# k and v of the first batch loaded into all 128 partitions instead of two half-partition pieces

## The chip, the cores and the metric

The kernel runs on one core of one Trainium2 chip. The metric is the device time of one execution in microseconds (us), the median over runs. The profile shows one execution, in us from the start of its span.

## What is computed

A linear attention with a norm over each head is followed by a token-mixing and a channel-mixing layer (a ResMLP block). Cut to what matters, with B = 8 batches, H = 8 heads, S = 576 tokens, D = 64:

```python
kv  = einsum('bhsd,bhse->bhde', k, v)              # per head, 64 x 64
o   = einsum('bhsd,bhde->bhse', q, kv)
o   = o / sqrt(mean(o*o, -1) + 1e-6) * g_norm
x   = o.transpose(0, 2, 1, 3).reshape(B, S, H*D)   # 8 x 576 x 512
a1  = alpha1 * x + beta1
u   = x + lam * einsum('ts,bsd->btd', w_tok, a1)
a2  = alpha2 * u + beta2
out = u + lam * (maximum(a2 @ w_ch1, 0) @ w_ch2)   # 512 -> 2048 -> 512
```

All inputs and the output are float32. q, k and v are each [8, 8, 576, 64].

## The kernel before

**One batch after the other.** For every batch the kernel makes kv for the eight heads, multiplies q by it, norms, mixes tokens (`tok_groups`), transposes (`ut_groups`) and runs the two channel products (`ch1_groups`, `ch2_groups`). While a batch is in its channel products, the next one is prepared. From batch 1 on, k and v come in one transfer of 1 MB each (`load_kv`), with 512 tokens over 128 partitions and 64 tokens in a tail tile.

**The first batch is different.** Its loads have no earlier batch to run beside, and they are cut into two halves of four heads, a = 0 and a = 1 (`HALVES`). `load_first(a)` (L508) loads k and v of a half. A head has 576 tokens, which are spread over 64 partitions with 9 tokens each, so a partition takes one unbroken piece of 9 x 64 floats (2304 bytes) of a head. `nine(tile, a, g)` (L463) is the view of that: partition half g of the tile holds two heads. Heads 4a and 4a+1 lie in partitions 0 to 63, heads 4a+2 and 4a+3 in partitions 64 to 127. Each (tile, a, g) is a transfer of its own, of 288 KB to 64 partitions: eight in all. The order of the loads on the SP queue is, for a = 0 and then a = 1: k (two transfers), v (two), q of the half (`load_main`, L493, 512 KB), and behind q of half 0 the last 64 tokens of q for all eight heads (`load_tail`, L500, 128 KB, into 64 partitions of `qft`). Then comes `moe_w_tok` (L1120, 1152 KB, and L1123, 144 KB).

**What the first batch does with it.** `kv_first` (L601) makes kv of a half: 36 small matmuls (72 instructions in the profile, since float32 takes two), each with 64 rows and 64 columns of the array, so that four of them sit in the array together. The head picks the rows (partition half of the input) and the columns (partition half of the PSUM output). ACT copies the results onto the diagonal blocks of `kv32` (L618): block r holds two heads, one in each partition half and column half. `qt_first` (L623) transposes q by matmuls with the identity: `pair(pr)` (L625, matmuls at L631) takes two heads into one block of `qt32`, `tail(a)` (L639, L645) takes the last 64 tokens. `qkv_groups` (L745) with `f32` (L767, matmuls at L771) then multiplies each block of `qt32` by the same block of `kv32`, 128 output columns for two heads at once, and writes them into PSUM side by side. Behind that follow the norm on ACT and DVE, and the transposes of `moe_w_tok` (`wt_groups`, L1151, matmuls at L1161), the token mix of batch 0 (`tok_first`, L905) and its transposes (L940), and the first channel product (L988).

**The order is made by a planner.** `Prog.op` records operations with an engine, an estimated cost, keys that are read and written, and for transfers an estimated `dma_us`. `Prog.schedule` (L169) is a list scheduler that runs them on its own clock and so fixes every engine's order when the program is built; `Prog.plan` (L122) repeats it eight times with other priorities and keeps the best. On its clock transfers pass through one pipe:

```python
dma_free = max(dma_free, t + 0.6) + pick.lat     # lat is dma_us
pick.end = dma_free + 2.0
```

**Filler matmuls.** As long as the first channel product has not started on the planner's clock, PE is never left idle in the plan: where no operation is ready, one filler matmul (`warm`, L1341 and L1342, 0.22 us on that clock) on a tile of zeros is written into PE's order. It is a fixed instruction: the chip runs it whether or not the data has come by then.

**The SP queue.** The loads are chained (`P.chain`), so they are issued in program order. `load_kv(1)` overwrites the buffers of half 0 and so waits for its matmuls; `load_q(1)` waits for the transposes of q.

Of the kernel before, what the change touches and what calls it, by code (L numbers as in the profile page):

```python
# [395 lines left out]
def bass_transnormer_attn__then__resmlp_affine_kernel(  # L396
# [15 lines left out]
    with ExitStack() as stack:  # L412
        P = Prog(nc, stack)

        def sb(name, shape, dt):
            return stack.enter_context(nc.sbuf_tensor(name, shape, dt))

        ident = sb("ident", [128, 128], F32)
# [23 lines left out]
        kv32 = kvd[:].rearrange("p h i d -> p (h i d)").bitcast(F32).rearrange(  # L442
            "p (r e) -> p r e", r=4)
# [16 lines left out]
        wst = hst[:, 0:2304].rearrange("p (c s) -> p c s", c=4)  # L460
        wst2 = hst[0:64, 2304:2880]

        def nine(tile, a, g):  # L463
            return tile[64 * g:64 * g + 64, a].rearrange("p h c d -> p (h c d)")[
                :, 0:1152].rearrange("p (h c d) -> p h c d", h=2, c=9)

        def flat(ap):
            return ap.rearrange("p h d -> p (h d)")
# [7 lines left out]
        def act_us(n):  # L476
            return 0.19 + n / 1200.0
# [4 lines left out]
        def act_dve(n, mode=1):  # L482
            return {"ACT": act_us(n), "DVE": dve_us(n, mode)}
# [4 lines left out]
        def copy(e, out, in_):  # L488
            if e is nc.scalar:
                return e.activation(out, in_, ACT.Identity)  # L490
            return e.tensor_copy(out=out, in_=in_)
# [8 lines left out]
        def load_tail(tile, key, src, b, lo, eng="SP"):  # L500
            P.op(eng, 0.6, lambda e: e.dma_start(
                tile[lo:lo + 64, :, :], src[b, :, 512:576, :].rearrange("h s d -> s h d")),
                w=[key], dma_us=0.75)

        HALVES = (slice(0, 4), slice(4, 8))
        ALL = (slice(0, 8),)

        def load_first(a):  # L508
            for key, src, tile in (("kf", k, kf), ("vf", v, vf)):
                for g in range(2):  # L510
                    P.op("SP", 0.45, lambda e, src=src, tile=tile, g=g: e.dma_start(
                        nine(tile, a, g).rearrange("p h c d -> p h (c d)"),
                        src[0, 4 * a + 2 * g:4 * a + 2 * g + 2].rearrange(
                            "h (p c) d -> p h (c d)", c=9)),
                        w=[(key, a)] if g == 0 else [(key + "g", a)], dma_us=1.05)

        def load_kv(b, go=()):
            j = (b + 1) % 2
            for tile, tl, src, n in ((kf, kft, k, "kf"), (vf, vft, v, "vf")):
                P.op("SP", 0.6, lambda e, tile=tile, src=src: e.dma_start(  # L520
                    tile[:, j].rearrange("p h c d -> p h (c d)"),
                    src[b, :, 0:512, :].rearrange("h (p c) d -> p h (c d)", c=4)),
                    r=go, w=[(n, j), (n + "g", j)], dma_us=3.8)
# [77 lines left out]
        def kv_first():  # L601

            def group(a):
                t = P.ptile(2)

                def f(e):
                    for c in range(9):
                        for h in (0, 2, 1, 3):
                            g, r = h // 2, slice(64 * (h % 2), 64 * (h % 2) + 64)
                            m = e.matmul(t.ap(r)[:, g, 0:64], nine(kf, a, g)[:, h % 2, c, :],  # L610
                                         nine(vf, a, g)[:, h % 2, c, :],
                                         start=(c == 0), stop=(c == 8), skip_group_check=True)
                    return m
                P.op("PE", 1.8, f, r=[(n, a) for n in ("kf", "kfg", "vf", "vfg")], w=[t])
                for h in range(2):
                    rows = slice(64 * h, 64 * h + 64)
                    P.op("ACT", act_us(128), lambda e, h=h, rows=rows: copy(
                        e, kv32[rows, 2 * a:2 * a + 2, 64 * h:64 * h + 64],  # L618
                        t.ap(rows)[:, :, 0:64]), r=[t, "kvz"], w=[("kv32", a, h)])
            for a in range(2):  # L620
                yield lambda a=a: group(a)

        def qt_first():  # L623

            def pair(pr):  # L625
                t = P.ptile(1)

                def f(e):
                    for c in range(4):
                        for h in range(2):  # L630
                            m = e.matmul(t.flat(slice(64 * h, 64 * h + 64))[  # L631
                                :, 128 * c:128 * c + 128], qf[:, 2 * pr + h, c, :], ident[:],
                                start=True, stop=True)
                    return m
                P.op("PE", 0.95, f, r=["ident", ("qf", pr // 2)], w=[t])
                P.op(act_dve(512), 0, lambda e: copy(e, qt32[:, pr, 0:512], t.flat()),
                     r=[t], w=[("q32", pr)])

            def tail(a):  # L639
                t = P.ptile(1)  # L640

                def f(e):
                    for pr in range(2):
                        h = 4 * a + 2 * pr
                        m = e.transpose(t.flat()[:, 64 * pr:64 * pr + 64],  # L645
                                        qft[0:64, h:h + 2, :].rearrange("p h d -> p (h d)"),
                                        ident[0:64, 0:64])
                    return m
                P.op("PE", 0.28, f, r=["ident", "qft0"], w=[t])
                P.op(act_dve(128), 0, lambda e: copy(  # L650
                    e, qt32[:, 2 * a:2 * a + 2, 512:576],
                    t.flat()[:, 0:128].rearrange("p (r s) -> p r s", r=2)),
                    r=[t], w=[("q32t", a)])
            for a in range(2):
                yield lambda a=a: pair(2 * a)
                yield lambda a=a: pair(2 * a + 1)
                yield lambda a=a: tail(a)
# [57 lines left out]
        def rows_of(b, c):  # L715
            return slice(0, 128) if c < 4 else slice(64 * (b % 2), 64 * (b % 2) + 64)
# [28 lines left out]
        def qkv_groups(b):  # L745

            def group(cs, hs):
                h0, nh, nc_ = hs.start, hs.stop - hs.start, len(cs)
                m = nc_ * nh
                t = P.ptile((m + 7) // 8)  # L750
                rows = rows_of(b, cs[0])
                nr = rows.stop - rows.start
                n = cnt["ch"]
# [13 lines left out]
                def f32(e):  # L767
                    a = h0 // 4
                    for i, c in enumerate(cs):
                        for j in range(2):  # L770
                            mm = e.matmul(  # L771
                                t.flat(rows)[:, 256 * i + 128 * j:256 * i + 128 * j + 128],
                                qt32[:, 2 * a + j, 128 * c:min(128 * c + 128, 576)],
                                kv32[:, 2 * a + j, :], start=True, stop=True)
# [15 lines left out]
                def split(ap):  # L790
                    if nc_ > 1:
# [11 lines left out]
                    r=[("sq", sqs)], w=[("sm", sms)], pri=-20)  # L803
# [4 lines left out]
                     r=[("sm", sms)], w=[("sm", sms)], pri=-200)  # L808
                lo, hi = 64 * h0, 64 * hs.stop
                x, r_ = xv(b, cs, lo, hi), rv(b, cs, lo, hi)  # L810
# [4 lines left out]
                else:  # L815
# [9 lines left out]
                     r=xk + ["e1"], w=[kk for c in cs for kk in rkeys(b, c, hs)], pri=-100, port=True)  # L825
# [297 lines left out]
        P.op("SP", 0.6, lambda e: e.dma_start(wst2, moe_w_tok[512:576, :]),  # L1123
             w=["wst2"], dma_us=0.6)
# [15 lines left out]
             w=["identb"])  # L1140
# [234 lines left out]
```

## Time and profile before

| | |
|---|---|
| median of 3 runs | 372.38 us (371.55 to 372.96) |
| the profiled execution | 371.84 us |
| its span in the profile | 370.0 us |
| granted TensorE clock | 1.00 |
| PE busy | 361.4 us (98%) |
| DVE busy | 200.9 us (54%) |
| ACT busy | 161.6 us (44%) |
| POOL busy | 82.1 us (22%) |
| HBM read and written | 38.56 MB and 9.44 MB |

The span is what the engines' records cover; the time of the execution is 1.84 us longer. Filler matmuls count as busy PE. The chain of work that ended last gives each piece with its start, its length and the instructions in it. In the table of stretches each row is a stretch of time with its length, the busy time of PE, PE's weight loads, DVE, ACT and POOL (with counts), the granted clock, the busy share of the DMA engines and the GB/s that they moved. A DMA row has the size and the time from issue to landing; SPq rows are the issue of a transfer on the SP queue.

### The profile page before, as it was taken

Reading aid. Unit: us, or ns where it says so; the run is one execution under the profiler, and the core shown is the slowest. Engines: PE = TensorE matmul, PEld = TensorE weight load, DVE = VectorE, ACT = ScalarE, POOL = GpSimd, SP = SyncE. Lnnn points to the kernel's source line nnn. Section 1 sums busy time; section 2 is a strip of 40 time slices with the busy share of each in tenths; the row PEclk is TensorE's granted clock in tenths of the full one; section 3 lists DMA queues with packets and bytes.
Section 4 is the critical chain, followed back from the end, with each engine's and each line's share of the span. In section 5 each row is a group of like instructions: output and inputs, shape, how many; then the busy total and the mean of one; then the engine's idle time right before and its main releaser. Section 6 shows DMA issues by size and latency. Waiting matters only on the chain.

```text
span 370.0 us, 7042 instructions
## 1 busy us (share of the span) xinstructions
PE 361.4 (98%) x3153; PEld 207.9 (56%) x2873; DVE 200.9 (54%) x302; ACT 161.6 (44%) x264; POOL 82.1 (22%) x69
## 2 busy tenths in 40 slices
PE   7999999999999999999999999999999999999995
PEld 3787656467754554456654554457654554457642
DVE  2377796982299279715937165925833175720021
ACT  1464886227850187008760188107730186007500
POOL 4043007340064008400341006200620007100000
PEclk9999999999999999999999999999999999999999
DMA  7999999889925893989954399233403110330021
GB/s 183 268 317 310 382 385 308 233 254 181 311 65 128 200 271 100 148 200 300 200 138 113 123 304 186 58 99 85 88 13 101 58 30 1 70 115 3 0 86 58
DMA packets 92295, 59.87 MB, mean 162 GB/s; under 512 B 59549, under 2 KB 82085, under 8 KB 92136
## 3 DMA queue, kind: packets, MB, share of 16 engines
q1 hardware_dynamic: 92240, 59.41, 61.6%
q8 instruction: 24, 0.39, 0.4%
q14 instruction: 7, 0.06, 0.1%
q10 hardware_dynamic: 24, 0.01, 0.0%
HBM read 38.56 MB, written 9.44 MB: 130 GB/s over the span
## 4 chain that ended last, share of the span: by engine, by line
PE 96%; ACT 2%; issue 0%; DVE 0%
PE ps L1025 34%; PE ps L1002 18%; PE ps L988 14%; PE ps L853 8%; PE ps L673 4%; PE ps L1342 3%; PE ps L764 2%; PE ps L390 2%; PE ps L875 1%; PE ps L771 1%; PE ps L905 1%; PE ps L940 1%; PE ps L631 1%; ACT qs L490 1%; ACT ht L978 1%; PE ps L610 1%
## 5 line engine op out<-in xcount | busy, mean ns | idle before, releaser
L1025 PE MATMUL ps<-w,ht 128*128 128x512 bf16 x576 | 129.7, 379 | 0.0
L978 ACT ACTIVATE ht<-ps,hb 128x512 bf16<-128x512 f32 (+1 forms) x128 | 93.4, 740 | 46.2 <-PE ps L1002 38.4
L828 POOL TENSOR_TENSOR xm<-xm,g_bc 128x512 f32<-128x512 f32 (+1 forms) x36 | 49.1, 1364 | 195.7 <-DVE rt L824 193.1
L1025 PEld LDWEIGHTS ps<-w,ht 128*128 128x128 bf16 x576 | 54.6, 98 | 64.3 <-issue 1.2
L1002 PE MATMUL ps<-a2t,w 128*128 128x320 bf16 x512 | 72.0, 299 | 1.4 <-ACT ht L978 1.4
L1002 PEld LDWEIGHTS ps<-a2t,w 128*128 128x128 bf16 x512 | 49.4, 98 | 21.9 <-ACT ht L978 1.9
L988 PE MATMUL ps<-a2t,w 128*128 128x512 bf16 x256 | 58.0, 379 | 0.0
L1035 DVE TENSOR_TENSOR xm<-ps,xm 128x512 f32<-128x512 f32 x32 | 21.7, 687 | 63.1 <-PE ps L1025 63.0
L700 ACT ACTIVATE kvd<-ps 64x128 bf16<-64x128 f32 x28 | 7.6, 271 | 98.0 <-PE ps L683 97.7
L801 DVE TENSOR_REDUCE small<-sq 128x16 f32<-128x1024 f32 (+3 forms) x27 | 25.2, 933 | 32.0 <-ACT sq L799 31.9
L988 PEld LDWEIGHTS ps<-a2t,w 128*128 128x128 bf16 x256 | 24.0, 98 | 26.9
L853 PE MATMUL ps<-rt,wt 128*128 128x512 bf16 x112 | 28.7, 379 | 0.0
L860 DVE TENSOR_TENSOR xm<-ps,xm 128x1024 f32<-128x1024 f32 x14 | 17.0, 1221 | 21.5 <-PE ps L853 21.4
L799 ACT ACTIVATE sq<-ps 128x1024 f32<-128x1024 f32 (+3 forms) x27 | 21.5, 797 | 8.1 <-PE ps L771 4.4
L824 DVE TENSOR_TENSOR rt<-xm,e1g_bc 128x1024 bf16<-128x1024 f32 (+1 forms) x18 | 21.3, 1182 | 0.1
L705 DVE TENSOR_TENSOR kvd<-ps,kvd 64x128 bf16<-64x128 f32 x28 | 8.1, 289 | 24.4 <-ACT kvd L700 23.8
L764 PEld LDWEIGHTS ps<-kvd,qt 128*128 128x128 bf16 x280 | 17.9, 98 | 3.9
L820 DVE TENSOR_TENSOR xm<-ps,small 128x1024 f32<-128x1024 f32 (+1 forms) x18 | 19.8, 1099 | 0.3
L564 DVE TENSOR_TENSOR qs<-qf,qs 128x2048 bf16<-128x2048 f32 (+1 forms) x10 | 17.7, 1787 | 3.1 <-ACT qs L490 3.0
L390 PE MATMUL ps<-kvd,qt 128*128 128x64 bf16 x280 | 19.0, 193 | 0.0
L764 PE MATMUL ps<-kvd,qt 128*128 128x64 bf16 x280 | 19.0, 193 | 0.0
L853 PEld LDWEIGHTS ps<-rt,wt 128*128 128x128 bf16 x112 | 11.0, 98 | 12.9 <-DVE xm L1035 0.2
(103 smaller groups left out, 287.9 us busy)
## 6 DMA issues: line engine op xcount, KB each, us to landing
out_dram<-xm SPq DMA_DIRECT2D x32, 256.0 KB, 2.6
kf<-in_k_dram SPq DMA_DIRECT2D x7, 1024.0 KB, 9.9
vf<-in_v_dram SPq DMA_DIRECT2D x7, 1024.0 KB, 9.7
qf<-in_q_dram SPq DMA_DIRECT2D x7, 1024.0 KB, 7.7
stg<-in_moe_w_ch_dram SPq DMA_DIRECT2D x3, 1024.0 KB, 14.5
kf<-in_moe_w_ch_dram SPq DMA_DIRECT2D x2, 1024.0 KB, 13.8
kf<-in_k_dram SPq DMA_DIRECT2D x4, 288.0 KB, 6.2
vf<-in_v_dram SPq DMA_DIRECT2D x4, 288.0 KB, 7.8
```

The source lines that it names most:

```text
L390: return pe.add_instruction(mybir.InstMatmult(start_tensor_calc=start, stop_tensor_calc=stop, tile_size=(128, 128), tile_position=(0, 0), ...
L764: e.matmul(o, w, kvd[:, h, 0, :], start=True, stop=False)
L799: P.op("ACT", act_us(64 * m), lambda e: e.activation(sqv, raw(), ACT.Square), r=[t], w=[("sq", sqs)])
L801: P.op("DVE", dve_us(64 * m), lambda e: e.tensor_reduce(out=smv, in_=sqv.rearrange("p (h d) -> p h d", h=m), axis=AX.X, op=ALU.add), r=[(" ...
L824: lambda e: e.tensor_tensor(out=r_, in0=x, in1=eb, op=ALU.mult),
L828: P.op("POOL", pool_us(64 * nh), lambda e, xc=xc: e.tensor_tensor(out=xc, in0=xc, in1=g_bc[rows, None, :].to_broadcast([nr, nh, DH]), op=A ...
L853: m = e.matmul(t.ap()[:, i, :], tok_w(b, sc, c), rsrc(b, sc), start=(sc == 0), stop=(sc == 4))
L978: o = P.op("ACT", act_us(n) + 0.09, lambda e: e.activation(dst, src(), ACT.Relu, bias=hb[:, fj:fj + 1]), r=[t, ("hb", fj // 4)], w=[("ht", ...
L988: m = e.matmul(t.flat(), w1[:, dj, 128 * fj:128 * fj + 128], a2t[:, dj, 0:512], start=(dj == 0), stop=(dj == 3))
L1002: m = e.matmul(t.ap()[:, i, 0:320], w1[:, dj, 128 * fj:128 * fj + 128], a2t[:, dj, 320 * i:320 * i + 320], start=(dj == 0), stop=(dj == 3))
L1025: m = e.matmul(t.flat(), ht[:, fj, 128 * c:128 * c + 128], w2[:, fj, :], start=(fj == 0), stop=(fj == 15))
L1035: P.op("DVE", dve_us(512), lambda e: e.tensor_tensor(out=x, in0=t.flat(), in1=x, op=ALU.add), r=[t] + keys, w=keys)
```

## The change

The two partition halves of the k and v tiles no longer hold two pairs of heads one above the other. Instead each head pair lies across the partitions: partition half y holds heads 4a + 2x + y for x = 0, 1. With that a whole tile of a half batch is one transfer to 128 partitions (576 KB, the same pieces of 2304 bytes), so four transfers take the place of eight. A kv block now holds heads 4a + y and 4a + 2 + y instead of two neighbours. So the transposes of q take the matching heads (`pair`), the last tokens of q are loaded with the heads in that order, in four transfers of two heads each instead of one of eight (`load_first_tail`, two behind q of each half), and the product `f32` writes its 128 columns as two runs of 64 that lie 128 columns apart, so that the heads are in order again in PSUM. The estimates for the planner change too: a k or v tile 0.6 us of issue and `dma_us` 1.6 (before: twice 0.45 and 1.05), a q tail 0.45 and 0.25 (before: 0.6 and 0.75, once).

```diff
-        def nine(tile, a, g):
-            return tile[64 * g:64 * g + 64, a].rearrange("p h c d -> p (h c d)")[
-                :, 0:1152].rearrange("p (h c d) -> p h c d", h=2, c=9)
+        def nine(tile, a):
+            return tile[:, a].rearrange("p h c d -> p (h c d)")[:, 0:1152].rearrange(
+                "p (x c d) -> p x c d", x=2, c=9)
...
         def load_first(a):
             for key, src, tile in (("kf", k, kf), ("vf", v, vf)):
-                for g in range(2):
-                    P.op("SP", 0.45, lambda e, src=src, tile=tile, g=g: e.dma_start(
-                        nine(tile, a, g).rearrange("p h c d -> p h (c d)"),
-                        src[0, 4 * a + 2 * g:4 * a + 2 * g + 2].rearrange(
-                            "h (p c) d -> p h (c d)", c=9)),
-                        w=[(key, a)] if g == 0 else [(key + "g", a)], dma_us=1.05)
+                P.op("SP", 0.6, lambda e, src=src, tile=tile: e.dma_start(
+                    nine(tile, a).rearrange("p x c d -> p x (c d)"),
+                    src[0, 4 * a:4 * a + 4].rearrange("(x y) (p c) d -> (y p) x (c d)",
+                                                      y=2, c=9)),
+                    w=[(key, a)], dma_us=1.6)
+
+        def load_first_tail(a):
+            for y in range(2):
+                P.op("SP", 0.45, lambda e, y=y: e.dma_start(
+                    qft[0:64, 4 * a + 2 * y:4 * a + 2 * y + 2, :],
+                    q[0, 4 * a + y:4 * a + y + 3:2, 512:576, :].rearrange("h s d -> s h d")),
+                    w=[("qft0", a, y)], dma_us=0.25)
...
@@ kv_first
                def f(e):
                     for c in range(9):
-                        for h in (0, 2, 1, 3):
-                            g, r = h // 2, slice(64 * (h % 2), 64 * (h % 2) + 64)
-                            m = e.matmul(t.ap(r)[:, g, 0:64], nine(kf, a, g)[:, h % 2, c, :],
-                                         nine(vf, a, g)[:, h % 2, c, :],
+                        for x, y in ((0, 0), (0, 1), (1, 0), (1, 1)):
+                            r = slice(64 * y, 64 * y + 64)
+                            m = e.matmul(t.ap(slice(64 * x, 64 * x + 64))[:, y, 0:64],
+                                         nine(kf, a)[r, x, c, :], nine(vf, a)[r, x, c, :],
                                          start=(c == 0), stop=(c == 8), skip_group_check=True)
...
@@ qt_first, pair
                             m = e.matmul(t.flat(slice(64 * h, 64 * h + 64))[
-                                :, 128 * c:128 * c + 128], qf[:, 2 * pr + h, c, :], ident[:],
+                                :, 128 * c:128 * c + 128], qf[:, 4 * (pr // 2) + 2 * h + pr % 2, c, :], ident[:],
...
@@ qt_first, tail
-                P.op("PE", 0.28, f, r=["ident", "qft0"], w=[t])
+                P.op("PE", 0.28, f, r=["ident"] + [("qft0", a, y) for y in range(2)], w=[t])
...
@@ qkv_groups, f32
                             mm = e.matmul(
-                                t.flat(rows)[:, 256 * i + 128 * j:256 * i + 128 * j + 128],
+                                t.flat(rows)[:, 256 * i:256 * i + 256].rearrange(
+                                    "p (x y d) -> p y x d", x=2, y=2)[:, j],
                                 qt32[:, 2 * a + j, 128 * c:min(128 * c + 128, 576)],
-                                kv32[:, 2 * a + j, :], start=True, stop=True)
+                                kv32[:, 2 * a + j, :].rearrange("p (x d) -> p x d", x=2),
+                                start=True, stop=True)
...
         for i, hs in enumerate(HALVES):
             load_first(i)
             load_q(0, hs, False)
-            if i == 0:
-                load_tail(qft, "qft0", q, 0, 0)
+            load_first_tail(i)
```

The keys of the later loads (`load_kv`, `load_tail`) follow the new names.

More of the change, by code (lines that the diff above doesn't have):

```diff
@@ L502, in load_tail @@
                 tile[lo:lo + 64, :, :], src[b, :, 512:576, :].rearrange("h s d -> s h d")),
-                w=[key], dma_us=0.75)
+                w=[key] + [("qft0", a, y) for a in range(2) for y in range(2) if lo == 0],
+                dma_us=0.75)
         HALVES = (slice(0, 4), slice(4, 8))
@@ L522, in load_kv @@
                     src[b, :, 0:512, :].rearrange("h (p c) d -> p h (c d)", c=4)),
-                    r=go, w=[(n, j), (n + "g", j)], dma_us=3.8)
+                    r=go, w=[(n, j)], dma_us=3.8)
                 for g in range(2):
@@ L607, in f @@
                     for c in range(9):
-                        for h in (0, 2, 1, 3):
-                            g, r = h // 2, slice(64 * (h % 2), 64 * (h % 2) + 64)
-                            m = e.matmul(t.ap(r)[:, g, 0:64], nine(kf, a, g)[:, h % 2, c, :],
-                                         nine(vf, a, g)[:, h % 2, c, :],
+                        for x, y in ((0, 0), (0, 1), (1, 0), (1, 1)):
+                            r = slice(64 * y, 64 * y + 64)
+                            m = e.matmul(t.ap(slice(64 * x, 64 * x + 64))[:, y, 0:64],
+                                         nine(kf, a)[r, x, c, :], nine(vf, a)[r, x, c, :],
                                          start=(c == 0), stop=(c == 8), skip_group_check=True)
                     return m
-                P.op("PE", 1.8, f, r=[(n, a) for n in ("kf", "kfg", "vf", "vfg")], w=[t])
+                P.op("PE", 1.8, f, r=[("kf", a), ("vf", a)], w=[t])
                 for h in range(2):
```

## The prediction

> **What bounds the kernel now.** I read first the page's chain by engine, then the table of stretches, then the chain in order of time over the first 40 us, and last the SP queue with its landings.
>
> ```profile
> span 370.0 us, 7042 instructions
> ...
> PE 96%; ACT 2%; issue 0%; DVE 0%
> ```
>
> ```profile
> 2.25:8.25 6.00, 6.00 (x23) 2.54 (x22) 0.43 (x2) 0.74 (x2) 2.80 (x6) 1.00 1.00 234
> 10.00:15.75 5.75, 5.75 (x104) 4.07 (x97) 1.36 (x6) 2.33 (x5) 0.00 (x0) 1.00 1.05 217
> 16.00:20.00 4.00, 3.79 (x95) 3.04 (x95) 2.61 (x7) 2.72 (x8) 0.00 (x0) 1.00 1.05 385
> 38.00:54.00 16.00, 15.51 (x187) 9.10 (x184) 14.08 (x30) 13.41 (x28) 0.00 (x0) 1.00 1.05 386
> 46.00:370.00 324.00, 317.98 (x2608) 176.95 (x2326) 174.29 (x245) 139.54 (x216) 70.21 (x47) 1.00 0.57 143
> ```
>
> The chain is 96% PE, and from 46 us on PE works 317.98 of 324.00 us. The edit touches nothing there. So the change is worth what it takes off the way to that dense stretch, and no more. In the start PE looks as busy, but much of it is filler:
>
> ```profile
> 1.86 5.55 PE ps L1342 x18
> 7.42 0.36 PE ps L1098 x2
> 7.78 1.83 PE ps L1342 x8
> 9.61 1.21 PE ps L610 x72
> 10.82 1.05 PE ps L1098 x2
> 11.87 1.90 PE ps L631 x32
> 13.77 0.39 PE ps L645 x4
> 14.15 0.15 PE ps L1074
> 14.31 0.54 PE ps L1342 x2
> 14.85 2.56 PE ps L771 x20
> 17.41 1.07 PE ps L610 x59
> 18.48 0.21 issue
> 18.69 0.45 PE ps L610 x13
> 19.14 0.54 PE ps L1342 x2
> 19.68 1.90 PE ps L631 x32
> 21.57 0.43 PE ps L771 x4
> 22.00 0.97 PE ps L1342 x4
> 22.97 1.78 PE ps L771 x16
> 24.76 0.47 PE ps L1161 x4
> ...
> 31.37 0.65 PE ps L1342 x3
> ```
>
> L1342 is filler: 26 matmuls before kv of half 0 (L610 at 9.61), then 0.54, 0.54 and 0.97 us up to the first transpose of `moe_w_tok` at 24.76, and 0.65 at 31.37. Fillers are written in where the planner, on its own clock, waits for a load or an evacuation.
>
> The reading that carries the most: in the stretches 2.25 to 8.25 and 10.00 to 15.75, in which mostly the 64-partition loads of k and v run, the DMA engines are fully busy (share 1.00 and 1.05) and move only 234 and 217 GB/s. In 16 to 20 us, with the end of q and then `moe_w_tok`, equally busy engines move 385; both go to 128 partitions. So the loads of k and v run at about 0.6 of the rate of their neighbours.
>
> **The loads.** Eight transfers of 288 KB (294,912 B) go, four of 576 KB come. Before, by the two rows, one took 294,912 / 234,000 = 1.26 us in half 0 and 1.36 in half 1. A load to 128 partitions in pieces of 2304 bytes is not in the trace. Bounds: 217 GB/s, no gain, if the pieces and not the partitions set the rate; 386 GB/s from the stretch 38 to 54, where weight rows of 512 floats (2048 bytes) are loaded to 128 partitions. I take 385, since that row has the nearest piece size and the same number of partitions: 589,824 / 385,000 = 1.53 us a tile. Up to v of half 0 that saves 4 x 1.26 - 2 x 1.53 = 1.98 us, up to `moe_w_tok` 4 x 1.26 + 4 x 1.36 - 4 x 1.53 = 4.36 us. The Trainium skill, page "SBUF — State Buffer", section "Door 1: The DMA port swizzle (why `[64,N]` ≈ `[32,N]`)", says that partitions 0 to 63 reach only 8 of 16 DMA ports, and gives 328 GB/s for 1 MiB on 128 partitions; by 328 a tile would take 1.80 us, and v of half 0 would land at 7.6 instead of the 7.1 below.
>
> The q tails: 128 KB in four transfers instead of one, the same pieces of 256 bytes and the same 64 partitions, so I count them at nothing; two of them now stand behind q of half 1, which takes half their bytes out of the way of k of half 1. The SP queue issues 12 transfers instead of 13, and it runs far ahead of the data, as the last of these rows shows:
>
> ```profile
> 2.87 0.63 SPq L511 DMA_DIRECT2D vf<-in_v_dram  x1
> vf<-in_v_dram SPq DMA_DIRECT2D x1, 288.0 KB, 6.2
> ...
> 19.61 1.73 PEld L631 LDWEIGHTS ps<-ident,qf 128*64 128x64 f32 x32 [0.42 <-DMA qf<-in_q_dram]
> ...
> 9.21 0.50 SPq L1123 DMA_DIRECT2D ht<-in_moe_w_tok_dram  x1
> ht<-in_moe_w_tok_dram SPq DMA_DIRECT2D x1, 144.0 KB, 14.0
> ```
>
> v of half 0 landed at 2.87 + 6.2 = 9.1, just ahead of PE's 9.6; q of half 1 was what PE waited for at 19.61; the end of `moe_w_tok` landed at 9.21 + 14.0 = 23.2, ahead of PE's 24.76. After the change these come at about 7.1, 15 and 18.8.
>
> **But PE does not follow the data.** It follows its written order, fillers included. So the question is how many fillers the planner now writes, and its estimates answer that; they give the order only, and what a filler costs comes from the chain's rows. On its clock v of half 0 landed at 0.6 + 4 x 1.05 + 0.15 for three small rows + 2.0 = 6.95 us; now it lands at 0.6 + 2 x 1.6 + 0.1 + 2.0 = 5.9. That is 1.05 us less to fill, 4 to 5 fillers at 0.22. In the profile eight took 1.83 us, 0.229 each: 4.5 x 0.229 = **1.03 us** off the way to L610, which starts at 8.6 instead of 9.61. The data is there at 7.1, a cover of 1.5 us; without that cover (the loads as slow as before) PE would wait until 9.1 again.
>
> From 9.61 to 24.76 the chain is 15.15 us, of which 0.54 + 0.54 + 0.97 are filler, 0.21 is issue, and 12.89 is work. The work stays instruction for instruction: kv (four 64 x 64 tiles of the array at once, the same pattern), the transposes and L771.
> - The 0.54 at 14.31 is filler until the q blocks of half 0 are evacuated. It stays, and since the second tail's transposes (0.39 / 2 = 0.20) move from here to half 1, it may be one filler longer.
> - The 0.54 at 19.14 is filler until q of half 1 lands. On the planner's clock that was at 16.25 and is now at 14.0 (two tiles less 2.0 us, half the tail 0.25), while PE's order there is kv of half 0, broadcast, transposes, product, kv of half 1 and reaches these transposes at about 14.9. So this filler goes: **0.54 us**. On the chip q lands at 15 and PE comes at about 19.68 - 0.54 - 1.03 = 18.1, so no wait takes its place.
> - The 0.97 at 22.00 is filler until the q blocks of half 1 are evacuated. The tail's transposes, 0.20, now stand in it, as does L771 x4 already; it shrinks, and with the filler at 14.31 I count the two at **0.2 us** less in sum, with bounds of -0.4 and 0.5.
>
> What is late next at 24.76 is `moe_w_tok`, at 18.8 against a PE that would come at 24.76 - 1.8 = 23.0. Cover: 4 us. Further on, everything queued behind in SP comes about 4.4 us earlier on the chip and 1.75 us earlier on the planner's clock (8 x 1.05 + 0.75 - 4 x 1.6 - 4 x 0.25), against a PE that is 1.6 earlier there, so I expect nearly the same order of work up to the first channel product.
>
> The strided output of L771 I count at nothing: the nearest rows have unbroken outputs, and here each run is still 64 floats. The upper bound is in the rivals.
>
> Sum: 1.03 + 0.54 + 0.2 = 1.77 us, and 0.2 to 0.3 for the issue gap of 0.21 and the filler of 0.65 at 31.37, which have some chance to go: **2.0 us**. On the profiled execution that is 371.84 - 2.0 = 369.8. The median before is 372.38, 0.54 above that execution, so I forecast 370.3 for the median. 0.5% (1.86 us) is about what a measurement of this kernel can tell from no change.
>
> **The rivals.**
>
> *More than that.* The loads 4.4 us earlier let the planner use the other fillers and stalls of the start too: the 0.65 at 31.37, the 0.97 at 22.00 in full. For it: that time is all filler. Against: both hang on evacuations and sums, not on loads. 2.0 + 0.45 + 0.77 is about 3.2 us: 369.2. Chance 0.15.
>
> *Hidden anyway.* Only the first fillers go; the rest of the start hangs on evacuations by ACT and DVE, and what is won at 19.14 is filled again at 22.00. For it: the 0.97 there is such a wait. It gives -1.03: 371.3. Chance 0.13.
>
> *The faster load is none.* The piece size sets the rate: the loads stay at 217 to 234 GB/s. Then PE, with fewer fillers, waits for v of half 0 at 9.1 and for q of half 1 at 19.3 as before, and little is won: 372.1. Against: 385 and 386 with pieces of like size. Chance 0.05.
>
> *The order turns against it.* q of batch 1 comes earlier and its split gets into DVE's order ahead of the last evacuation of the transposes, on which the first channel product waits.
>
> ```profile
> 37.66 0.75 DVE L950 TENSOR_SCALAR a2t<-ps,ab 128x512 bf16<-128x512 f32 x1 [0.49 <-PE ps L940]
> 38.32 0.75 DVE L491 CAST qs<-qf 128x512 bf16<-128x512 f32 x2
> 38.99 1.28 DVE L564 TENSOR_TENSOR qs<-qf,qs 128x512 bf16<-128x512 f32 x2
> ```
>
> The split stands right behind it today, a margin of 0.66 us. By the planner's clock that margin shrinks by only 0.15 (1.75 against 1.6). If it is used up, 0.75 + 1.28 = 2.03 us come before L950, once for each half of q: between 2.03 and 4.1 us lost, net between 372.4 and 374.5. Chance 0.12, of which I put two thirds beyond 0.5%.
>
> *Slower: L771 pays for its broken output.* The 40 instructions (rows of 2.56, 0.43 and 1.78) take 4.77 us, 0.119 each. If a matmul whose output runs are 128 columns apart cost twice as much, 4.77 us would be added, net +2.8: 375.2. It cancels the gain from 0.05 us more per matmul, and is slower by 0.5% from 0.10. The Trainium skill, page "PSUM — Partial Sum Buffer", section "Specifications (TRN2)", says of its 8-byte lines that any non-contiguous access pattern slows matmuls significantly; by that rule this case would hold. The trace has no matmul with a broken output, and no run here shows the rule; the jump comes only once in 64 floats. Chance 0.10.
>
> **How the numbers follow.** Chances: forecast 0.45, more 0.15, hidden 0.13, order 0.12, broken output 0.10, no faster load 0.05. Faster by over 0.5% (below 370.5): all of "more" and 0.33 of the forecast, whose own range is 369.4 to 371.2, makes 0.48. Slower by over 0.5% (above 374.2): 0.10 + 0.08 = 0.18. Within: 0.34. The range takes in all but the broken output and the ends of the others: 368.6 to 374.5.
>
> **What would show it.** Right: L610 starts near 8.6 with 21 or 22 fillers ahead of it; the stretch of the k and v loads moves over 330 GB/s; no filler ahead of the second L631 group; the first L1161 near 23.0; L771 x20 still near 2.56 us; and the dense stretch as long as before. Wrong: DMA named as the releaser of L610 or L631 with a long wait; L771 near 5 us; DVE rows of the q split ahead of L950; or a start that is 2 us shorter and a dense stretch that is longer, which would mean that the planner's order lost elsewhere what was won here.

## The result

| | before | after |
|---|---|---|
| median of 20 runs each, same chip | 372.30 us | 373.12 us |
| range of the runs | 371.3 to 372.96 | 372.11 to 373.58 |
| span of the profiled execution | 370.0 | 371.3 |

The ratio after to before is 1.0017, with a 95% interval of 1.001 to 1.0024: the change costs 0.17%, which lies within the 0.5% that I had named as no change. The forecast was 370.3, so it was 2.8 us too low and had the wrong sign; the range of 368.6 to 374.5 holds the time.

The page of after, its first line and its chain by engine:

```profile
span 371.3 us, 7052 instructions
...
PE 97%; ACT 1%; DVE 0%; issue 0%
```

PE bounds the kernel as before. The table of stretches of after, with the columns of the prediction's table (length, busy time and count on PE, PEld, DVE, ACT and POOL, granted clock, share of the DMA engines, GB/s):

```profile
2.25:8.25 6.00, 6.00 (x19) 2.38 (x18) 2.07 (x4) 0.78 (x2) 2.79 (x6) 1.00 1.01 327
10.00:12.00 2.00, 2.00 (x60) 1.18 (x51) 0.00 (x0) 0.73 (x3) 0.00 (x0) 1.00 1.10 369
...
46.00:371.30 325.30, 319.32 (x2635) 177.85 (x2353) 170.47 (x240) 139.04 (x215) 72.28 (x48) 1.00 0.56 139
```

The last column is what the change was about: 327 and 369 GB/s in the stretches of k and v (the first also holds q of half 0 and its tails), where it was 234 and 217. From 46 us to the end PE idles 325.30 - 319.32 = 5.98 us, against 6.02 before. So no wait was won or lost there; what changed lies ahead of it. The issues on the SP queue (start, length) and the transfers of v of half 0, q of half 1 and the end of `moe_w_tok` (last number: us from issue to landing):

```profile
1.24 0.45 SPq L511 DMA_DIRECT2D vf<-in_v_dram  x1
vf<-in_v_dram SPq DMA_DIRECT2D x1, 576.0 KB, 4.9
4.85 0.49 SPq L494 DMA_DIRECT2D qf<-in_q_dram  x1
qf<-in_q_dram SPq DMA_DIRECT2D x1, 512.0 KB, 9.6
7.55 0.49 SPq L1131 DMA_DIRECT2D ht<-in_moe_w_tok_dram  x1
ht<-in_moe_w_tok_dram SPq DMA_DIRECT2D x1, 144.0 KB, 11.7
```

They landed at 1.24 + 4.9 = 6.1, 14.5 and 19.3 us; before at 9.1, about 19.6 and 23.2. The data came 3 to 5 us earlier, and the kernel was not faster. The chain of waits of after in order of time (start, length, line, count) shows what PE did instead. L1350 is the filler (L1342 before), L617 the first kv product (L610), L638 and L652 the transposes of q, L778 the product `f32` (L771), L1169 the first transpose of `moe_w_tok` (L1161), L997 the first channel product (L988):

```profile
1.86 3.60 PE ps L1350 x8
...
6.08 3.44 PE ps L1350 x14
9.51 1.21 PE ps L617 x72
...
14.09 0.97 PE ps L1350 x4
15.06 1.21 PE ps L617 x72
16.27 1.09 PE ps L778 x8
17.36 2.07 PE ps L638 x32
19.43 1.67 PE ps L778 x12
...
21.36 0.32 PE ps L1350
...
24.05 0.68 PE ps L1169 x4
...
25.40 0.75 PE ps L1350 x3
26.16 0.47 PE ps L1169 x4
26.62 0.86 PE ps L1350 x4
...
38.79 0.32 PE ps L1350
...
39.99 1.73 PE ps L1350 x8
41.71 0.86 PE ps L997 x4
```

Read the places at which the stages begin. The first kv product starts at 9.51 (before 9.61): 0.1 won. The first transpose of `moe_w_tok` starts at 24.05 (24.76): 0.7 won. The first channel product starts at 41.71; before it stood at 39.18, so from transpose to channel product PE took 17.66 us where it had taken 14.42. The fillers in that part are 0.75 + 0.86 + 0.32 + 1.73 = 3.66 us, where the only ones before were the 0.65 at 31.37: 3.01 of the 3.24 us more. Another 0.39 is work of batch 1 (L690, ahead of 38.79) that used to come behind the first channel product. Over the whole profiled execution the fillers of the chain sum to 11.99 us instead of 10.08; PE is busy 363.5 us instead of 361.4 and idle 7.8 instead of 8.6, which makes the 1.3 us between the spans. And the order is another one: the kv product of half 1 (15.06) now runs ahead of L778 of half 0 and of q's transposes, and the groups of L1169 are pulled apart. The data arrived, and the planner wrote another program around it.

### The profile page after: what moved, and what is told of

It is laid out like the page before. It is cut to its first block, busy times and chain, and to the rows that moved or that the text cites. A ratio compares the mean times of both kernels' runs of the same rounds, so it can differ in the third digit from the quotient of the medians.

```text
span 371.3 us, 7052 instructions
## 1 busy us (share of the span) xinstructions
PE 363.5 (98%) x3159; PEld 209.0 (56%) x2879; DVE 195.0 (53%) x293; ACT 162.6 (44%) x266; POOL 90.6 (24%) x76
## 4 chain that ended last, share of the span: by engine, by line
PE 97%; ACT 1%; DVE 0%; issue 0%
PE ps L1034 34%; PE ps L1011 18%; PE ps L997 15%; PE ps L862 8%; PE ps L680 4%; PE ps L1350 3%; PE ps L771 2%; PE ps L390 2%; PE ps L778 1%; PE ps L884 1%; PE ps L914 1%; PE ps L949 1%; PE ps L638 1%; PE ps L690 1%; PE ps L1169 1%; PE ps L617 1%
## 5 line engine op out<-in xcount | busy, mean ns | idle before, releaser
L997 PE MATMUL ps<-a2t,w 128*128 128x512 bf16 x256 | 58.7, 379 | 0.0
L997 PEld LDWEIGHTS ps<-a2t,w 128*128 128x128 bf16 x256 | 23.9, 98 | 26.2
L771 PEld LDWEIGHTS ps<-kvd,qt 128*128 128x128 bf16 x280 | 18.0, 98 | 4.1
L833 DVE TENSOR_TENSOR rt<-xm,e1g_bc 128x1024 bf16<-128x1024 f32 (+1 forms) x17 | 19.8, 1169 | 0.1
L771 PE MATMUL ps<-kvd,qt 128*128 128x64 bf16 x280 | 19.1, 193 | 0.0
L571 DVE TENSOR_TENSOR qs<-qf,qs 128x2048 bf16<-128x2048 f32 (+1 forms) x8 | 16.4, 2060 | 1.5 <-ACT qs L490 1.4
```

The source lines that it names most:

```text
L771: e.matmul(o, w, kvd[:, h, 0, :], start=True, stop=False)
L997: m = e.matmul(t.flat(), w1[:, dj, 128 * fj:128 * fj + 128], a2t[:, dj, 0:512], start=(dj == 0), stop=(dj == 3))
```

## The experiments

Each kernel was timed against the kernel before on the same chip; ratios are to it. I had three questions: what are the loads worth by themselves, what is the new order worth by itself, and what makes the new order fill so much.

**The loads in the old order.** The k and v tiles go to 128 partitions as in the change, but as eight transfers of 288 KB with the old estimates, and all q tails behind q of half 0, so that the planner writes the order of before for the engines. The product `f32` has its broken output.

```diff
-                P.op("SP", 0.6, ... nine(tile, a) ... w=[(key, a)], dma_us=1.6)
+                for x in range(2):
+                    P.op("SP", 0.45, ... nine(tile, a)[:, x] ... dma_us=1.05)
```

> The loads of the change with the order of before on every compute engine: k and v go to all 128 partitions, but as eight transfers of one head pair (288 KB) with the planner's old estimates, and all q tails stand behind q of half 0. Theory A (the written order, not the data, sets the start): the loads run at 330 GB/s or more and land 2 to 4 us earlier, yet PE stays within 0.5 us of before at its first product of kv and at the first transposes of w_tok; time between -0.6 and 0 us against before. Theory B (the faster loads are worth 2 us and the new order takes them back): -1.5 to -2.5 us. Theory C (the broken output or the new pairing costs by itself): +0.5 us or more, with L771's group longer than before.

Measured: 372.48 us, ratio 0.9998 (0.9985 to 1.001). The loads alone changed nothing. The chain of this kernel, with the filler at L1353 and `f32` at L779:

```profile
1.86 6.73 PE ps L1353 x18
...
8.95 1.83 PE ps L1353 x8
10.79 1.21 PE ps L618 x72
...
16.02 2.56 PE ps L779 x20
...
22.23 0.43 PE ps L779 x4
...
23.63 1.78 PE ps L779 x16
```

No piece of the start is a DMA. PE works off its 26 fillers, 18 and 8, which stand in its order for the landing that the planner assumes, and v, which landed at 2.1 + 5.4 = 7.5 us, is nowhere what it waits for. The first kv product starts at 10.79, 1.2 us behind that of before and not within the 0.5 us expected: in this execution the first 18 fillers took 6.73 us instead of 5.55 (see the last section). The three rows of `f32` are 2.56, 0.43 and 1.78 us, to the hundredth those of L771 before: the broken output costs nothing.

**The order by itself.** The loads of before, with estimates that bring them on the planner's clock as early as in the change, and the q tail in two; the engines' order is that of after.

```diff
-                        w=[(key, a)] if g == 0 else [(key + "g", a)], dma_us=1.05)
+                        w=[(key, a)] if g == 0 else [(key + "g", a)], dma_us=0.8)
```

> The order of the change on every compute engine with the loads of before: eight half-partition transfers with the planner told 0.8 each, the q tail in two transfers of four heads. Theory A: the order costs, and the late data now adds to it: v of half 0 lands at about 9 us as before, but the half-1 data that the new order wants at 15 to 17 us lands at 16.8 and 19.3, so +2 to +4 us against before. Theory B: the same sign, +2 us over the change itself. Theory C (the new form costs): about the time of before, within 0.5 us.

Measured: 374.89 us, ratio 1.0086 (1.0055 to 1.0118). Its profiled execution was an exceptionally long one (span 377.1; it raises the ratio too), so only the kind of wait is read from it, not its size:

```profile
6.88 11.23 DMA vf<-in_v_dram
18.15 2.20 PE ps L616 x72
```

The order with slow loads waits for v of half 1 ahead of its early kv product. By the medians it loses 374.89 - 372.36 = 2.5 us against before; with the fast loads it loses 0.8. So the fast loads are worth 374.89 - 373.12 = 1.8 us in this order and 0 in the old one with its fillers. That spoke for fillers that hide the loads.

**The fillers shortened.** The loads in the old order once more, with every filler behind the sixteenth cut to 64 columns; it stays in its place in the order and takes almost no time. Beside it, the kernel before with the same short fillers.

```diff
-            return e.matmul(t.flat(), wz[:, 0:128], wz, start=True, stop=True)
+            P.fed += 1
+            n = 512 if P.fed <= 16 else 64
+            return e.matmul(t.flat()[:, 0:n], wz[:, 0:128], wz[:, 0:n], start=True, stop=True)
```

> The loads alone with the old order (as in the first of these runs), and every filler behind the 16th writes 64 columns instead of 512: PE can follow the data. If the loads are worth what the prediction said, and only the fillers hid it: kv of half 0 at 7.5 to 8.5 us, q blocks of half 1 without a DMA wait, first transposes of w_tok at about 22, time -1.5 to -2.5 us against before. If the start hangs on the evacuations and the norm chain anyway: less than -0.8 us. To be read beside the next run, which has the same fillers and the old loads.

> The kernel before with the same short fillers behind the 16th. The old loads land v of half 0 at 9.1 and q of half 1 at 19.3 us, so DMA should now be named as releaser of the first kv product and of the q transposes of half 1, in the place of the fillers: 0 to -0.6 us against before. If it gains as much as the run with the new loads (more than -1.5 us), the fillers are the cost and the loads are worth nothing in any order.

Measured: 368.42 us with the new loads, ratio 0.9895 (0.9879 to 0.991), and 370.55 with the old ones, 0.9948 (0.9934 to 0.9961). The loads are worth 370.55 - 368.42 = 2.1 us here, and 0 with long fillers (the first experiment). Both kernels won more than was expected of them, 3.8 us instead of 1.5 to 2.5 and 1.7 instead of 0 to 0.6: the long fillers cost 1.7 us even with the slow loads. First the chain with the new loads, with filler L1356 and the first channel product L999:

```profile
1.86 5.69 PE ps L1356 x18
...
19.53 0.22 PE ps L1356 x4
...
28.47 0.09 PE ps L1356 x3
...
35.72 0.90 PE ps L999 x4
```

The fillers that took 0.97 and 0.65 us take 0.22 and 0.09, and the first channel product starts at 35.72 instead of 39.18. The same view with the old loads:

```profile
2.87 6.75 DMA vf<-in_v_dram
...
12.00 3.51 PE ps L632 x32
```

Here the fillers are gone and a DMA takes their place: v of half 0, landing at 9.6. (This execution was 0.8 us above its median, and 1.6 us of its start are the slow L632, of which more below; so the worth of the loads is taken from the medians.) The version with the new loads beats both kernels, the one before by 1.05%: the change's placement of k and v, the order of before, and short fillers.

**The same with the change's own transfers.** Four of 576 KB as in the change, in the old order but for one parameter's broadcast, which comes ahead of the first kv product; the rest as in the version above.

```diff
-                P.op("SP", 0.6, lambda e, src=src, tile=tile: e.dma_start(
+                P.op("SP", 1.05 if key == "kf" else 0.75, lambda e, src=src, tile=tile: e.dma_start(
...
-                    w=[(key, a)], dma_us=1.6)
+                    w=[(key, a)], dma_us=2.1)
```

> The change's own four transfers of 576 KB (not eight of 288 KB) with the old order and short fillers behind the 16th; the q tails stand behind q of half 0, and one broadcast of a parameter row comes ahead of the first kv product instead of behind it. If the partitions and not the size of a transfer give the rate: within 0.5 us of the fastest such run with eight transfers (368.42), so 1.0% faster than before. If the bigger transfers are better or worse by themselves: outside of that, with v of half 0 landing before or after.

Measured: 368.97 us, ratio 0.9929 (0.9906 to 0.9951). The median is 0.55 us above the version with eight transfers, a shade outside what was expected. Seven of the eleven runs lie at 368.3 to 369.2 and four at 371.1 to 371.7, those with a mean granted clock of 0.994 or 0.995 instead of 0.997 or more. v of half 0 landed at 1.26 + 4.7 = 6.0 us, 1.5 us ahead of the version with eight transfers, but nothing came of it: the first kv product starts at 9.30 (8.2 there), since the broadcast that now stands ahead of it waits for DVE:

```profile
8.18 1.12 PE L1108 MATMUL ps<-xm,ones 1*128 1x512 f32 x2 [0.59 <-DVE xm L1094]
```

So what the earlier landing could win is not shown. With the change's own transfers the kernel is faster than before all the same; the order and the fillers are what the change lost by.

**Eight long fillers instead of sixteen**, in the version with 368.42:

```diff
-            n = 512 if P.fed <= 16 else 64
+            n = 512 if P.fed <= 8 else 64
```

> The loads alone with the old order as in the fastest run so far, with only 8 fillers of full size instead of 16: the clock has less work to come up, and the g broadcast and the first kv product come about 2 us sooner, at the landing of v (about 7 us). If the fillers' number sets the start: -0.5 to -1.5 us against that run (368.42). If the rows of the parameters, v and the evacuations set it by now, or the slow start of the matmuls returns: within 0.5 us, or slower.

Measured: 367.57 us, ratio 0.9899 (0.9861 to 0.9937). Four of six runs lie at 366.8 to 367.6, two at 370.9 and 371.3. Now PE waits 1.1 us for v of half 0. Fewer fillers win 0.9 us in most runs and lose 2.5 to 3 in some, so this is not shown to be better. The four big transfers, whose v landed 1.5 us earlier, were not run with eight long fillers.

**Where the new order fills.** The kernel after, fillers behind the first kv product cut to 64 columns:

```diff
-            return e.matmul(t.flat(), wz[:, 0:128], wz, start=True, stop=True)
+            n = 64 if P.fed else 512
+            return e.matmul(t.flat()[:, 0:n], wz[:, 0:128], wz[:, 0:n], start=True, stop=True)
```

> The change with its order, but each filler behind the first kv product writes 64 columns instead of 512 (21 fillers, 4.6 us of them in the profile of the change). Theory D (fillers are dead time, they hold up ready work): -1.5 to -3 us against the change. Theory E (they only cover waits for evacuations and PSUM banks): -0.8 us or less, with the same wait now shown as idle PE in their place.

Measured: 371.44 us, ratio 0.9979 (0.9968 to 0.999); after itself had 1.0017. So fillers were 0.38% of it (1.7 us by the medians, between what the two theories expected), but the first channel product, at 40.69, is still far from 35.72. What stands in the fillers' place are waits on ACT and DVE, here in the order of time on PE (in brackets the idle time before, and what ended it):

```profile
26.68 1.66 PE L1171 MATMUL ps<-ident,ht 128*128 128x128 f32 x12 [0.39 <-DVE xm L831]
...
40.69 0.60 PE L999 MATMUL ps<-a2t,w 128*128 128x512 bf16 x2 [1.15 <-ACT a2t L960]
```

The first row is odd: transposes of `moe_w_tok` (L1171) wait for the multiply of the norm (L831), from which they take no data. They share a PSUM bank with its input. In the bank assignment that the planner writes into the program, five of the eight banks hold half products that wait for the norm on ACT and DVE at that time, two hold transposes, and one the fillers. In the old order the kv product of half 1 came only after L771 of half 0 (17.41 behind 14.85 in the prediction's rows). The second row is the last evacuation ahead of the channel product. ACT in the kernel after, in order of time, shows why it is late:

```profile
37.62 1.26 ACT L958 ACTIVATE a2t<-ps,ab 128x512 bf16<-128x512 f32 x2 [3.54 <-PE ps L949]
...
38.86 0.55 ACT L707 ACTIVATE kvd<-ps 64x128 bf16<-64x128 f32 x2
39.44 0.63 ACT L490 ACTIVATE qs<-qf 128x512 bf16<-128x512 f32 x1
40.09 0.27 ACT L707 ACTIVATE kvd<-ps 64x128 bf16<-64x128 f32 x1
40.27 0.67 ACT L958 ACTIVATE a2t<-ps,ab 128x512 bf16<-128x512 f32 x1
```

The last `a2t` (L958, 40.27) stands behind the q split and the kvd copies of batch 1. In the old order the q split came behind it (DVE, 38.32 behind 37.66). Two experiments took these two places away one by one.

**One more bank.** As the last kernel, but with the fillers behind the first kv product left out, and the third group of those transposes in the bank that they had used:

```diff
+        ft = P.warm[3]
+        gone = {x for x in P.sequence if ft in x.tiles and x.start > P.kv0.start}
+        P.sequence = [x for x in P.sequence if x not in gone]
...
+        t2.bank = fb
```

> The change with its order, no filler at all behind the first kv product, and the PSUM bank that the fillers held given to the third group of w_tok transposes, which in the written order takes over the bank of a half-1 product and so waits until the norm on DVE has read it. To be read beside the run with small fillers. If the bank is what holds that group up: it starts right behind the second group, 0.5 to 0.8 us earlier than there (26.68), with no DVE row as its releaser; time -0.2 to -0.7 us against the run with small fillers if the start follows, 0 if the next wait (the copies of the transposes, the sums) takes it back.

Measured: 371.5 us, ratio 0.9972 (0.9962 to 0.9983). The transposes come in five groups of four. In the last kernel the second group started at 25.42, and the third is the head of the row at 26.68. Here the third follows the second without a gap, in the first of these rows:

```profile
24.95 1.23 PE L1175 MATMUL ps<-ident,ht 128*128 128x128 f32 x8
26.38 1.19 PE L1175 MATMUL ps<-ident,ht 128*128 128x128 f32 x8 [0.21 <-ACT wt L493]
```

So the third group starts at about 25.5, 1.1 us earlier, of which 0.47 was won ahead of the second. The multiply of the norm is gone as a releaser: the bank was the wait at that place. The next wait is for a bank again. The fourth group, at 26.38, takes over the bank of the second, which ACT has to copy out first (L493). The first channel product stands at 40.15 instead of 40.69. The time differs by less than the interval from the 0.9979 of the kernel with short fillers, so its price is not settled.

**The evacuation first.** The kernel with short fillers, the last `a2t` on ACT moved ahead of the batch-1 work in front of it:

```diff
+        for x in P.sequence:
+            if x.eng == "ACT" and pe < x.start < last.start and x not in P.uta:
+                x.start = last.start + 0.01 + 0.001 * (x.start - pe)
```

> The change with its order and small fillers, but on ACT the last evacuation of the transposed tokens of batch 0 goes ahead of 1.17 us of work for batch 1 (a q cast and two kv copies) that stood before it. If that work holds up the first channel product: it starts at 40.0 to 40.3 instead of 40.69, -0.3 to -0.7 us against the run with small fillers. If the channel product waits for something else, or batch 1 pays later: within 0.2 us.

Measured: 372.56 us, ratio 1.0002 (0.9992 to 1.0011), 1.1 us slower than without the move; neither a gain nor "within 0.2 us", as was expected. The first channel product does come earlier, at 40.20, but the second one at 59.93 instead of 59.18. Within it PE has two waits that the kernel with short fillers does not have:

```profile
43.75 0.62 PE L597 MATMUL ps<-identb,qs 128*128 128x128 bf16 x8 [0.56 <-ACT ht L993]
44.75 0.61 PE L597 MATMUL ps<-identb,qs 128*128 128x128 bf16 x8 [0.38 <-DVE qs L574]
```

L597 are the transposes of q of batch 1. The first of them wait for the relu of the channel product (`ht`), from which they take no data; by the program's bank assignment it empties the bank that they take over, and on ACT it now comes behind the moved work. The second wait for their input, the split of q. What was won ahead of the channel product was given back within it, and more.

**The planner's estimates alone.** Three kernels change only what the planner believes: after with `dma_us` of a k or v tile at 1.1 instead of 1.6, the same with the fillers behind the sixteenth cut to 64 columns, and before with 1.1 instead of 1.05.

```diff
-                    w=[(key, a)], dma_us=1.6)
+                    w=[(key, a)], dma_us=1.1)
```

> The change with one number altered: the planner is told 1.1 instead of 1.6 for a k or v tile, so that it writes another order (fewer fillers before the first channel product: 25 instead of 43 in all). Loads, sizes and instructions are the same. Theory A: the time follows the order: first channel product 2 to 4 us earlier than in the change (38 to 40 us in the span), time -1.5 to -3 us against the change, so 0.2 to 0.6% faster than before. Theory B' (the data sets it, and the too early order only waits for transfers): DMA named as releaser of PE, time within 0.5 us of the change.

> The change with the estimate 1.1 and short fillers behind the 16th. That order has 5 fillers of full size left behind the first kv product (1.2 us in its profile), so if fillers are dead time -0.5 to -1.2 us against the same order with full fillers (370.55), if they cover waits within 0.3 us of it.

> The kernel before with one number altered: the planner is told 1.1 instead of 1.05 for each half load of k and v. Nothing else differs but the order that comes out, which on the planner's own clock ends 3.5 us later. If the order is as touchy as theory A says, the time is +1 to +4 us against before, more than the whole change makes; if the planner's clock says little about the chip, within 0.5 us.

Measured: 370.55 us, ratio 0.996 (0.9946 to 0.9974); 370.87, 0.9951 (0.9935 to 0.9967); 372.96, 1.0018 (1.0008 to 1.0027). The first is 1.8 us below the kernel before and 2.6 below the kernel after, from which it differs by one number that changes no transfer: a third order, with the first transpose of `moe_w_tok` at 22.90 and the first channel product at 38.93. The second shows that in this order the fillers cover waits, since shortening them wins nothing that can be measured. The third moves one estimate of the kernel before by 5% and costs 0.7 us, as much as the whole change, though less than the 1 to 4 us expected.

## Why the prediction was wrong

**Right, step by step.** The rate in kind: 327 and 369 GB/s instead of 234 and 217, with 385 forecast (327 is just short of the 330 that was named as a sign). The landings: 6.1, 14.5 and 19.3 us, with 7.1, 15 and 18.8 forecast. The count of 22 fillers ahead of the first kv product. No wait for q of half 1. The `f32` product as long as before (2.56, 0.43 and 1.78 in the same order), against the rule on the page "PSUM — Partial Sum Buffer" of the Trainium skill, section "Specifications (TRN2)", which this run does not bear out for runs of 64 floats. The dense stretch with the same idle time. The refuted rivals are so the load that is no faster and the broken output. The sum of 2.0 us is met in size by the 2.1 that the loads are worth with the order held and the fillers short. That is partly luck: the terms of the forecast were fillers that the planner would leave out, and what goes in the measured pair is a wait of PE for v.

**The step that failed** is the sentence "so I expect nearly the same order of work up to the first channel product". I had derived it from two sums on the planner's clock (data 1.75 us earlier, PE 1.6 earlier) as if such a shift left the order as it was. And both sums hold only behind the last of these loads. At v of half 1 the same estimates give 8 x 1.05 + 0.75 - 4 x 1.6 - 2 x 0.25 = 2.25 us for the data, against 1.05 for the first kv product on PE. The planner made another order from there on: the kv product of half 1 came forward, half products piled up in PSUM, batch-1 work came ahead of the last evacuation, and 17.66 us followed where there had been 14.42, with 3.66 us of filler instead of 0.65. The rival "the order turns against it" had the mechanism of the second half of this, with the q split and kvd copies ahead of the last `a2t` (on ACT, not on DVE), and too small a chance (0.12); its margin argument used the same false step. That PSUM banks would become the wait was in no rival.

**The mis-sized terms.** The first fillers were to give 1.03 us and gave 0.1. I counted 4.5 removed fillers at 0.229 us, the pace of the last eight; but the first fillers are slower, and the eight that now stand ahead of L1107 (the broadcast of a parameter row, L1098 before) take 3.60 us, 0.45 each. L1107 itself, still at that pace, takes 0.62 us instead of 0.36, and its weight load comes 0.84 us behind the one before it:

```profile
5.39 0.50 PEld L1107 LDWEIGHTS ps<-xtl,ones 1*128 1x128 f32 x2 [0.84 <-issue]
```

How long PE stays slow differs from execution to execution, so 0.1 is what one pair shows. In the four traced executions with these 22 fillers (after, small fillers, one more bank, evacuation first) the first kv product starts at 9.51, 9.84, 9.85 and 9.73; in two with 26 (before, loads alone) at 9.61 and 10.79. What four fillers are worth is not settled by them.

The fillers behind the first kv product were right in sum, by chance: 0.54, 0.54 and 0.97 us became 0.97 and 0.32, which is 0.76 less with 0.74 forecast, though at other places. Of the 1.1 us between 24.05 and the forecast 23.0, 0.9 are the first fillers in this pair.

What stays open: how much of the 3.2 us is the banks and how much the evacuations. Both places are shown; taking away the first alone moved the wait and hardly the time, and taking away the second alone made the kernel slower.

## What to carry to other kernels

Where a planner writes the order, an edit of its estimates is an edit of the whole program: compare the order of instructions before pricing anything by the old trace, and to price a transfer hold the order still. Filler work that was sized for slow data can hide fast data completely, as it did here, so faster loads and shorter fillers had to come together (0.9998 and 0.9948 alone, 0.9895 together). A wait for an engine from which no data comes was a shared PSUM bank in the three places where it was followed up here; look for who holds it.

## What the runs showed of the hardware

The first matmuls run slowly, for a time that differs from execution to execution. The same 18 fillers took 5.55 us before, 6.37 in before with the estimate of 1.1, and 6.73 in the first experiment. PE's weight loads, in order of time, show the pace. First in the kernel with four big transfers, the last slow one and the row behind it:

```profile
4.40 0.15 PEld L1355 LDWEIGHTS ps<-a2b 128*128 128x128 bf16 x1 [0.28 <-issue]
4.75 2.04 PEld L1355 LDWEIGHTS ps<-a2b 128*128 128x128 bf16 x10 [0.20 <-issue]
```

The same two in the first experiment:

```profile
6.96 0.15 PEld L1353 LDWEIGHTS ps<-a2b 128*128 128x128 bf16 x1 [0.28 <-issue]
7.35 0.75 PEld L1353 LDWEIGHTS ps<-a2b 128*128 128x128 bf16 x4 [0.24 <-issue]
```

Until 4.75 and 7.35 us the fillers come one every 0.43 us, behind that about one every 0.2. The granted clock reads 1.00 for 2.25 to 8.25 us in all of them, as it does in the tables of before and after. The Trainium skill, page "TensorE: Matmul & The Clock Gate", section "What's actually happening", says that the array starts at half its clock and is released at the end of a free-running window of 3.4 us, so that the count of slow matmuls differs from run to run. The traces agree in the pace and in that the end of the slow time moves, here by 7.35 - 4.75 = 2.6 us. For the same 18 fillers that made 1.2 us between two executions, more than the 0.8 us that the change cost.

The pace can also fall again. With the old loads and short fillers, PE waited 1.99 us for v of half 0 (the 6.75 us of DMA above), and the 32 transposes L632 behind it took 3.51 us instead of 1.90, in this stretch of that kernel (third number from the end: the granted clock):

```profile
12.00:15.60 3.60, 3.60 (x35) 3.37 (x35) 0.00 (x0) 1.24 (x3) 0.00 (x0) 0.55 1.06 227
```

A granted clock of 0.55 over 3.6 us cost 1.6 us in that execution. A wait of 1.1 us for v, in the profiled execution with eight long fillers, was not followed by such a fall: the 32 transposes took 1.90 us there. The four high runs with big transfers and one of the two with eight long fillers show a lower mean clock and may have the same cause; their starts were not traced, and the other of the two shows a mean clock of 1.0.
